# Weight sums of a seven-product matrix multiplication, moved from VectorE to accumulating DMAs

## The chip, the cores and the metric

The kernel runs on one core of one Trainium2 chip. The metric is the time of one execution on the device, in microseconds (us). The engines are TensorE (PE, with its weight loads shown apart as PEld), VectorE (DVE), ScalarE (ACT), GpSimd (POOL) and SyncE (SP), which issues the DMAs of the kernel before. The trace has one profiled execution; its rows are in us or ns.

## What is computed

The reference is block attention over 16 heads' worth of (2, 8, 768, 64) queries, keys and values, and then two feed-forward layers on the 1536 resulting rows of 512:

```python
attn = softmax([local window of 16 | block maxima of k + log 32]) @ [v | block means of v]
x = attn.transpose(0, 2, 1, 3).reshape(1536, 512)
g, val = x @ w_gate, x @ w_val                 # 512 -> 1536
y = (g * sigmoid(g) * val) @ w_out             # 1536 -> 512
h = y @ w_in                                   # 512 -> 2048
out = piecewise(h) @ w_out2                    # h, 0 or (h + 1)^2 / 4;  2048 -> 512
```

The weights come as 64-bit floats and are decoded on the chip to float32. Each float32 product is made of three matmuls: an operand is split into a rounded high part and a low part (value minus high part), and high x high, high x low and low x high are added.

## The kernel before

The 1536 rows are worked on in three chunks of 512. A planner (`Plan.emit`, lines 127 on) takes jobs with needs, buffer rings, engine costs and a rank, and emits them one after the other: always the ready job with the least start time plus 0.00016 x rank. So the constants in `T` set the order on every engine, and each engine then runs its own queue in that order. Where the planner expects PE to idle, `bank` puts padding transposes of `ident` ahead of a job (line 296).

Attention runs first (0 to some 175 us), mixed with the layers of chunk 0, which use the ordinary form (to 265 us). Decoded weights are written to DRAM (`kept_g`, `kept_i` and others). The first products of either layer for chunks 1 and 2 (`JOINT`) are then made together by a seven-product form: the two chunks and two halves of the inner dimension give 2x2 blocks, and seven block products with sums of blocks take the place of eight. Stage 1 has six groups of weights (gate and value columns), stage 2 has four; a group has two quads (e = 0, 1) of seven forms of six matmuls each.

For one group, `read_group` (line 1193) loads a buffer `wj` of 128 x 2 x 4 x 256 values in two DMAs, and `add_group` (line 1208) makes a buffer `sj` of the same size, four sums of 128x512 on DVE, by the table `SUMS` in line 1206: first 0 and 2 from the loaded blocks, then 1 from sum 0, then 3 from sum 1. `wj` and `sj` share a ring of three buffers (`raw`). `group_hi` and `group_lo` (lines 1220, 1226) split both into high and low parts (`wjo` from the plain blocks, `wjs` from the sums; a ring of four, `wA`). PE's job `form` (line 1306) multiplies them with the blocks of x and their differences (`TERMS`, line 1265, split by `term_hi` and `term_lo`) and `fork` and `join` (lines 1318, 1322) build the outputs from the seven products. The second products of each layer (`row_jobs`, tile `acc_y`) use row weights that are read back from DRAM (`wf`, line 1411) and split; they can run at any time after their hidden values are there, so the planner fills PE with them.

Of the kernel before, what the change touches and what calls it, by code (L numbers as in the profile page):

```python
# [23 lines left out]
T = {'rings': {'sm': 4, 'raw': 3, 'dd': 2, 'wf': 3, 'wA': 4, 'h': 3},  # L24
 'handoff': 0.3,
 'urge': 0.00016,
 'weight': (0.925, 772.894, 0.282, 0.289),
 'order': ((0, 1), (0, 2)),
 'pack': 2,
 'ahead': '',  # L30
 'd': (-5637.212, 41085.045),
 'load': (3008.479, 4747.053),
 'high': (-2836.042, 3239.532),
 'bits': (-935.349, 1886.602),
 'keep': (-57947.518, -5594.531),
 'read': -11449.662,
 'hi': (-27701.488, 1102.421),
 'lo': (-11590.763, -2406.109),
 'head_rank': (5076.154, -7290.563, -60395.485, -15458.656),
 'half_rank': -29616.131,  # L40
 'start': 464.292,
 'unit': 1.932,
 'e0': 462.563,
 'a1': (62.363, 14.301),
 'a2': (116.213, 16.636),
 'x': (617.322, 3982.825),
 'j': (2797.217, 10463.422),
 'g': (1.248, 6.748),
 'q': (0.007, 0.113),
 'jr': (1234.441, 846.231),  # L50
 'jw': (1404.409, 766.537),
 'rw': 858.964,
 'js': (-6034.078, 1900.145),
 'gh': (746.555, 1544.378),
 'gl': -1712.874,
 't': 484.136,
 'th': 822.2,
 'tl': -35.6,
 'qp': (-30.096, -19.417, -3.899, 35.81, 32.684, -24.767, -40.513),
 'qf': -562.767,  # L60
 'qj': -1653.995,
 'qa': 2416.954,
 'rs': 3036.454,
 'rh': 887.986,
 'x2': 255.064,
 'r2': (400.241, 30033.282),
 'first': (-5645.576, -144.845),
 'st_q': (-2034.21, 345.71),
 'st_qt': (-732.561, -1914.119),
 'st_sc': (-685.966, -444.589),  # L70
 'st_mx': (-35663.85, -1356.97),
 'st_ex': (-3778.03, 3307.182),
 'st_iv': (-5276.379, 81.698),
 'st_no': (742.266, -11947.766),
 'st_wt': (-4363.695, 165.258),
 'st_pt': (-52297.254, -1058.814),
 'st_av': (-394.819, -213.378),
 'st_xh': (133.16, 1680.548),
 'st_xl': (-10069.461, -3131.586),
 'kl': (-42181.744, 4874.082),  # L80
 'kp': (3666.397, -5596.737),
 'kt': (-3814.781, -1844.408),
 'km': (-77721.471, 514.179),
 'kc': (2433.202, -51674.2),
 'vl': (-198.108, 134.248),
 'vm': (2794.065, -1853.404),
 'vs': 26403.355,
 'vo': (-29543.71, -26442.98),
 've': (-15678.039, 5229.978),
 'ql': (-31980.946, -7672.979),  # L90
 'wl': (-16312.191, -27195.823),
 'wide': 4,
 'st_su': (-4928.084, -22611.06),
 'seg': (-751.648, 28.239),
 'ko': (-4507.859, 33394.294)}


class Plan:
# [28 lines left out]
    def emit(self):  # L127
# [22 lines left out]
        while ready:  # L150
            best = None
            for name in ready:
                engines, rank, fn, needs, takes, gives, after, _ = jobs[name]
                chosen, start0 = [], after
                for group in takes:
                    times = [(t, i) for i, r in enumerate(group)
                             if (t := free_at(r, chosen.count(r))) is not None]
                    if not times:
                        break
                    now = max(start0, max((end[x] for x in needs), default=0.0))  # L160
                    early = [i for t, i in times if t <= now]
                    t, i = (0.0, early[0]) if early else min(times)
                    start0 = max(start0, t)
                    chosen.append(group[i])
                if len(chosen) < len(takes):
                    continue
                way = None
                for kind, us in engines.items():
                    engine, port = kind.strip("+"), kind == "POOL" or kind[-1] == "+"
                    start = max(start0, free.get(engine, 0.0))  # L170
                    if engine == "DMA":
                        us = us[0]
                    elif engine == "PE":
                        now = name[0] in self.TILED
                        start += self.SWITCH * (small and not now) + self.LEAD * (now and not small)
                    if port:
                        start = max(start, free.get("port", 0.0))
                    if engine == "DMA" and len(landed) >= self.LANES:
                        start = max(start, landed[-self.LANES])
                    for x in needs:  # L180
                        start = max(
                            start, end[x] + (self.HANDOFF if done_on[x] != engine else 0.0)
                        )
                    cost = start + self.WEIGHT.get(kind, 0.0) * us
                    if way is None or cost < way[0]:
                        way = cost, start, engine, us, port
                _, start, engine, us, port = way
                late = start + self.URGE * rank
                if best is None or late < best[0]:
                    best = late, start, name, engine, us, port, chosen  # L190
# [9 lines left out]
            if engine == "DMA":  # L200
                us, size, parts = jobs[name][0]["DMA"]
                at = start
                for _ in range(parts):
                    if len(landed) >= self.LANES:
                        at = max(at, landed[-self.LANES])
                    at += us / parts
                    free["moved"] = max(at + self.DMA_START, free.get("moved", 0.0)) + size / parts
                    landed.append(free["moved"] + self.DMA_END)
                free["DMA"], end[name] = at, landed[-1]
            elif engine == "PE":  # L210
                small = name[0] in self.TILED
            done_on[name] = engine
# [19 lines left out]
def tile_block_attention_ffn(  # L232
# [24 lines left out]
    P = 128  # L257
# [945 lines left out]
                    out=t[:, j].rearrange("p (u b) x -> p u (b x)", u=2),  # L1203
                    in_=kept["i", 4 * i + 2 * j])

    SUMS = {0: (0, 1, ALU.add), 2: (2, 0, ALU.subtract), 1: (4, 2, ALU.subtract), 3: (3, 5, ALU.subtract)}

    def add_group(st, i, s, engine):
        w = plain[st, i]
        if s == 0:  # L1210
            sums[st, i] = wp.tile(
                [P, 2, 4, 256], F32, tag="raw", name="sj", bufs=plan.rings["raw"])
        both = [w[:, :, x] if x < 4 else sums[st, i][:, :, x - 4] for x in SUMS[s][:2]]
        nc.vector.tensor_tensor(
            sums[st, i][:, :, s], *both, op=SUMS[s][2])

    def group_source(what, st, i, e):
        return plain[st, i][:, e, 1:4] if what == "o" else sums[st, i][:, e]
# [11 lines left out]
    def group_jobs(st, i, t):  # L1230
        names = [("keep", *group_units(st, i, 0)), ("keep", *group_units(st, i, 1))]
        if st == 1:
            names = [("keep", "g", 2 * i), ("keep", "g", 2 * i + 1)]
        n = (st, i)
        behind = [("load", len(packs) - 1) if n == (1, 0) else ("js", *prior_group, 0)]
        prior_group[:] = n
        job(("ja", *n), {"DMA": (0.8, 2.8, 2)}, t, lambda *_: read_group(st, i), names, (("raw",),),
            follows=behind)
        for s, (x, y, _) in SUMS.items():
            needs = [("ja", *n)] + [("js", *n, z - 4) for z in (x, y) if z >= 4]  # L1240
            job(("js", *n, s), {"DVE+": 0.7}, t + T["js"][st - 1],
                lambda e, *_, s=s: add_group(st, i, s, e), needs, (("raw",),) if s == 0 else (),
                follows=[("js", *n, 0)] if s == 2 else [])
        for e in range(2):
            for what, us in (("o", (0.86, 0.57, 0.97)), ("s", (1.07, 0.7, 1.23))):
                needs = [("ja", *n)] if what == "o" else [("js", *n, s) for s in SUMS]
                gives = ([(("ja", *n), 0)] if what == "o" else [(("js", *n, 0), 0)])
                m = (what, *n, e)
                rank = t + T["q"][st - 1] * e + T["gh"][what == "s"]
                job(("gh", *m), {"ACT": us[0], "DVE+": us[1]}, rank,  # L1250
                    lambda eng, *_, a=m: group_hi(*a, eng), needs, (("wA",),),
                    follows=prior("gh", ("gh", *m)) or [("hi", len(packs) - 1)])
                job(("gl", *m), {"DVE+": us[2]}, rank + T["gl"],
                    lambda eng, a=m: group_lo(*a, eng), [("gh", *m)], (), gives)

        for s in (1, 3):
            jobs = plan.jobs["js", *n, s]
            plan.jobs["js", *n, s] = (*jobs[:5], jobs[5] + ((("ja", *n), 0),), *jobs[6:])

    def operand(st, k, b):  # L1260
# [2 lines left out]
        return parts_of[st, k, b]  # L1263

    TERMS = {
        3: ((C2, 0), (C1, 0)), 5: ((C2, 1), (C2, 0)), 4: ((C2, 1), 3), 6: ((C1, 1), 4),
    }

    def add_term(st, k, b, engine, ring):
# [6 lines left out]
    def term_hi(st, k, b, engine):  # L1276
        if (st, k) not in xts:
            xts[st, k] = big.tile([P, 7, 2, CH], F32R, tag=f"big{k}", name=f"xj{k}")
        copy(engine, xts[st, k][:, b, 0], operand(st, k, b))

    def term_lo(st, k, b, engine):
        t = xts[st, k]
        subtract(engine, t[:, b, 1], operand(st, k, b), t[:, b, 0].bitcast(F32))

    def term_jobs(st, k, t, before, slots):
# [34 lines left out]
        copy(engine, t, quads[q, "a"])  # L1320

    def join(q, what, src):
        nc.vector.tensor_tensor(quads[q, what], quads[q, what], quads[q, src], op=ALU.add)

    def quad_jobs(q, t, slots):
        st, i, e = q
# [163 lines left out]
```

## Time and profile before

| | us |
|---|---|
| median of three runs (614.2 to 615.57) | 614.93 |
| span of the profiled execution | 612.5 |
| PE busy in it | 600.7 |
| DVE busy | 502.4 |
| ACT busy | 347.4 |
| POOL busy | 26.8 |

Busy time of PE counts matmuls back to back; matmuls overlap, so the mean length of one (some 389 ns) is longer than its share of busy time. The granted clock is given as a part of full speed: 1.00 is 2.4 GHz, 0.50 is 1.2 GHz. The DMA share is the mean busy share of the 16 DMA engines; it can pass 1 by rounding of the packets' times.

### The profile page before, as it was taken

What the parts mean: (1) busy time and instruction counts of PE and PEld (TensorE: products, weight loads), DVE (VectorE), ACT (ScalarE), POOL (GpSimd) and SP (SyncE); (2) the same over time, 40 slices, a digit from 0 to 9 for tenths busy, and PEclk for the clock granted to TensorE, in tenths of its full rate; (3) what the DMA queues carried; (4) which work ended last, traced back from release to release, by engine and by line L of the source; (5) the groups of instructions that cost most, each with busy time, mean ns of one, the idle gap of its engine ahead of it and who ended that gap; (6) DMA issues with size and microseconds to landing.
All of it is one profiled execution on the core that took longest, in us unless ns stands there. A gap on an engine that the chain in (4) does not pass through costs nothing.

```text
span 612.5 us, 9841 instructions
## 1 busy us (share of the span) xinstructions
PE 600.7 (98%) x3737; PEld 498.4 (81%) x3737; DVE 502.4 (82%) x910; ACT 347.4 (57%) x634; POOL 26.8 (4%) x54
## 2 busy tenths in 40 slices
PE   8699999999999999999999999999999999999997
PEld 7589888778888888888888888888888888888886
DVE  4788999989899898887788877788888897886662
ACT  5787687877979576454443433322268554742112
POOL 3320201000000000000000000000000000000000
PEclk9979999999999999999999999999999999999999
DMA  8999996999896398132110211123300131103411
GB/s 228 291 303 279 328 303 251 327 266 317 315 339 206 138 307 309 71 139 68 70 68 1 103 70 68 35 104 102 138 20 16 34 138 35 36 0 116 160 35 69
DMA packets 79199, 95.01 MB, mean 155 GB/s; under 512 B 36272, under 2 KB 62128, under 8 KB 79152
## 3 DMA queue, kind: packets, MB, share of 16 engines
q1 hardware_dynamic: 79152, 94.39, 47.9%
q8 instruction: 29, 0.48, 0.3%
q14 instruction: 18, 0.15, 0.1%
HBM read 73.40 MB, written 20.97 MB: 154 GB/s over the span
## 4 chain that ended last, share of the span: by engine, by line
PE 96%; DMA 1%; SPq 1%; ACT 1%; POOL 0%; issue 0%; ACTq 0%; POOLq 0%
PE acc_y L987 38%; PE qi L987 12%; PE qv L987 9%; PE qg L987 9%; PE pi L987 7%; PE pv L987 6%; PE pg L987 6%; PE px L588 2%; PE sc L637 2%; PE pt L683 1%; DMA raw<-in_moe_w_val_dram 1%; PE pk L518 1%; SPq L442 1%; PE pq L569 1%; PE pk L296 1%; SPq L884 1%
## 5 line engine op out<-in xcount | busy, mean ns | idle before, releaser
L987 PE MATMUL acc_y<-dd,h 128*128 128x512 f32 (+1 forms) x387 | 88.4, 387 | 0.0
L987 PEld LDWEIGHTS acc_y<-dd,h 128*128 128x128 f32 x387 | 72.4, 188 | 14.9
L987 PE MATMUL acc_y<-h,dd 128*128 128x512 f32 x288 | 66.1, 389 | 0.0
L987 PEld LDWEIGHTS acc_y<-h,dd 128*128 128x128 f32 x288 | 54.1, 188 | 11.2
L385 ACT ACTIVATE dd<-wf 128x1024 fp32r<-128x1024 f32 x25 | 26.4, 1057 | 61.3 <-PE acc_y L987 61.3
L987 PE MATMUL qi<-xj,wjs 128*128 128x512 f32 x192 | 46.4, 389 | 0.0
L987 PE MATMUL acc_y<-wA,h 128*128 128x512 f32 x192 | 45.8, 389 | 0.0
L903 DVE SCALAR_TENSOR_TENSOR wb<-dd 128x1024 int32<-128x1024 int32 x34 | 41.6, 1227 | 2.3 <-ACT dd L385 1.4
L926 DVE TENSOR_TENSOR wA<-wb,wA 128x1024 fp32r<-128x1024 f32 x34 | 41.6, 1231 | 1.8 <-ACT wA L385 1.1
L987 PE MATMUL pi<-y,wA 128*128 128x512 f32 x128 | 42.4, 392 | 0.0
L987 PEld LDWEIGHTS qi<-xj,wjs 128*128 128x128 f32 x192 | 36.0, 188 | 7.5
L987 PEld LDWEIGHTS acc_y<-wA,h 128*128 128x128 f32 x192 | 36.0, 188 | 7.5
L894 ACT ACTIVATE dd<-raw 128x1024 f32<-128x1024 f32 x34 | 38.8, 1144 | 1.4 <-DMA raw<-in_moe_w_val_dram 1.3
L987 PE MATMUL acc_y<-h,wA 128*128 128x512 f32 x144 | 36.5, 399 | 0.0
L987 PE MATMUL qg<-xj,wjs 128*128 128x512 f32 x144 | 36.4, 389 | 0.0
L987 PE MATMUL qv<-xj,wjs 128*128 128x512 f32 x144 | 36.2, 389 | 0.0
L987 PE MATMUL pg<-x,wA 128*128 128x512 f32 (+1 forms) x112 | 35.2, 371 | 0.0
L987 PE MATMUL qi<-xj,wjo 128*128 128x512 f32 x144 | 34.9, 389 | 0.0
L926 DVE TENSOR_TENSOR dd<-wf,dd 128x1024 fp32r<-128x1024 f32 x28 | 34.2, 1224 | 0.3 <-ACT dd L385 0.2
L987 PE MATMUL pv<-x,wA 128*128 128x512 f32 (+1 forms) x112 | 34.3, 369 | 0.0
L926 DVE TENSOR_TENSOR h<-r,h 128x512 fp32r<-128x512 f32 x47 | 32.4, 692 | 2.1 <-ACT h L385 0.7
L385 ACT ACTIVATE dd<-raw 128x1024 int32<-128x1024 uint32 x28 | 31.9, 1140 | 0.0
(163 smaller groups left out, 1198.8 us busy)
## 6 DMA issues: line engine op xcount, KB each, us to landing
raw<-in_moe_w_out_dram SPq DMA_DIRECT2D x14, 1024.0 KB, 6.3
raw<-in_moe_w_in_dram SPq DMA_DIRECT2D x16, 512.0 KB, 7.3
wf<-kept_z SPq DMA_DIRECT2D x16, 512.0 KB, 3.2
raw<-in_moe_w_gate_dram SPq DMA_DIRECT2D x12, 512.0 KB, 7.1
raw<-in_moe_w_val_dram SPq DMA_DIRECT2D x12, 512.0 KB, 7.6
kept_g<-wb SPq DMA_DIRECT2D x12, 512.0 KB, 5.6
wj<-kept_g SPq DMA_DIRECT2D x12, 512.0 KB, 4.3
wf<-kept_o SPq DMA_DIRECT2D x12, 512.0 KB, 3.2
```

The costliest lines, as they stand in the source:

```text
L296: nc.tensor.transpose(t[:, 0:P], ident, ident)
L385: nc.scalar.activation(out, in_, AF.Copy, scale=scale)
L442: nc.sync.dma_start(out=vwin[0:KW, w], in_=bass.AP(src.tensor, src.offset, [[D, KW], [S * D, H], [1, D]]),)
L518: nc.tensor.matmul(cols[h * D:(h + 1) * D, r], kraw[b, p][one, h, r], ident[one, one], start=True, stop=True, skip_group_check=True)
L569: nc.tensor.transpose(pq[:, r * P:(r + 1) * P], raw[:, r].rearrange("p h d -> p (h d)"), ident)
L588: nc.tensor.matmul(px[h * D:(h + 1) * D, col:col + QT], vwin[0:KN, w, 2 * p + h], pT[0:KN, 2 * h + w // 2, w % 2 * QT:(w % 2 + 1) * QT], s ...
L637: nc.tensor.matmul(scs[h][j * QT:(j + 1) * QT, w // 2], qT[head, (w + j) * QT:(w + j + 1) * QT], kwin[p][head, s * WPS + w + j], start=Tru ...
L683: nc.tensor.transpose(pt[0:KN, w * P:(w + 1) * P], v_["sm"][:, w], ident)
L894: nc.scalar.activation(x[:, 0], raws[k][:, :, :, 1].bitcast(F32), AF.Prelu, scale=2.0 ** -112, alpha=2.0 ** 32)
L903: nc.vector.scalar_tensor_tensor(b, x[:, 0], 3, x[:, 1], op0=ALU.logical_shift_left, op1=ALU.bitwise_or)
L926: e.tensor_tensor(out, a, b, op=ALU.subtract)
L987: nc.tensor.matmul(dst, lhs(a), rhs(b), start=first and i == 0, stop=last and i == 2, **more)
```

## The change

The sums of a group are no longer made on DVE. `read_sums` loads the starting values of `sj` from DRAM with SP's queue (4 DMAs in stage 1, 8 in stage 2), and `add_group` issues from POOL's queue one accumulating DMA per sum that adds a block of `wj` or an earlier sum in place. Since such a DMA only adds, differences are turned into sums: the signs go to the x blocks (terms 0 and 2 are negated, term 5 is turned around) and to the joins. The job `js` becomes an entry of its own in the planner (`SWD`), and nearly all constants of `T` are others.

```diff
+            elif engine == "SWD":
+                at = start + us + self.DMA_START
+                free["moved"] = max(at, free.get("moved", 0.0)) + jobs[name][0]["SWD"][1]
+                end[name] = free["moved"] + self.DMA_END
...
-    SUMS = {0: (0, 1, ALU.add), 2: (2, 0, ALU.subtract), 1: (4, 2, ALU.subtract), 3: (3, 5, ALU.subtract)}
+    SUMS = {0: 1, 2: 0, 1: 4, 3: 5}
+
+    def read_sums(st, i):
+        t = sums[st, i] = wp.tile(
+            [P, 2, 4, 256], F32, tag="raw", name="sj", bufs=plan.rings["raw"])
+        for s, (j, z) in enumerate(((0, 0), (1, 0), (1, 0), (1, 1))):
+            part = slice(256 * z, 256 * z + 256)
+            if st == 1:
+                nc.sync.dma_start(out=t[:, :, s], in_=kept["g", 2 * i + j][:, :, part])
+                continue
+            for e in range(2):
+                nc.sync.dma_start(out=t[:, e, s], in_=kept["i", 4 * i + 2 * e][:, j, part])
+
+    def add_group(st, i, s):
+        x = SUMS[s]
+        nc.gpsimd.dma_start(
+            out=sums[st, i][:, :, s],
+            in_=plain[st, i][:, :, x] if x < 4 else sums[st, i][:, :, x - 4], accum_op=ALU.add)
...
-        for s, (x, y, _) in SUMS.items():
-            needs = [("ja", *n)] + [("js", *n, z - 4) for z in (x, y) if z >= 4]
-            job(("js", *n, s), {"DVE+": 0.7}, t + T["js"][st - 1],
-                lambda e, *_, s=s: add_group(st, i, s, e), needs, (("raw",),) if s == 0 else (),
-                follows=[("js", *n, 0)] if s == 2 else [])
+        job(("jb", *n), {"DMA": (1.6 * st, 1.6 * st, 4 * st)}, t + T["js"][st - 1],
+            lambda *_: read_sums(st, i), names, (("raw",),), follows=[("ja", *n)])
+        for s, x in SUMS.items():
+            needs = [("ja", *n), ("jb", *n)] + ([("js", *n, x - 4)] if x >= 4 else [])
+            job(("js", *n, s), {"SWD": (1.2, 1.2)}, t + T["js"][st - 1],
+                lambda e, s=s: add_group(st, i, s), needs)
...
-        3: ((C2, 0), (C1, 0)), 5: ((C2, 1), (C2, 0)), 4: ((C2, 1), 3), 6: ((C1, 1), 4),
+        3: ((C2, 0), (C1, 0)), 5: ((C2, 0), (C2, 1)), 4: ((C2, 1), 3), 6: ((C1, 1), 4),
...
-        copy(engine, xts[st, k][:, b, 0], operand(st, k, b))
+        copy(engine, xts[st, k][:, b, 0], operand(st, k, b), -1.0 if b in (0, 2) else 1.0)
 
     def term_lo(st, k, b, engine):
         t = xts[st, k]
+        if b in (0, 2):
+            nc.vector.scalar_tensor_tensor(
+                t[:, b, 1], operand(st, k, b), -1.0, t[:, b, 0].bitcast(F32),
+                op0=ALU.mult, op1=ALU.subtract)
+            return
...
-        nc.vector.tensor_tensor(quads[q, what], quads[q, what], quads[q, src], op=ALU.add)
+        t = quads[q, what]
+        if what == "u2":
+            nc.vector.scalar_tensor_tensor(t, t, -1.0, quads[q, src], op0=ALU.mult, op1=ALU.subtract)
+        elif what == "s1":
+            nc.vector.tensor_tensor(t, quads[q, src], t, op=ALU.subtract)
+        else:
+            nc.vector.tensor_tensor(t, t, quads[q, src], op=ALU.add)
```

Of the constants, those that weigh the engines and some of the ranks that the prediction speaks of:

```diff
- 'weight': (0.925, 772.894, 0.282, 0.289),
+ 'weight': (0.935, 3248.959, 0.334, 0.207),
- 'load': (3008.479, 4747.053),
+ 'load': (3040.175, 4777.003),
- 'jr': (1234.441, 846.231),
+ 'jr': (364.158, 292.817),
- 'first': (-5645.576, -144.845),
+ 'first': (-5979.904, 282.679),
- 'vl': (-198.108, 134.248),
+ 'vl': (-1507.519, -2239.376),
- 'wl': (-16312.191, -27195.823),
+ 'wl': (-12671.815, 7162.137),
```

## Rows read from the trace of the kernel before

**Rows 1.** The page: busy us, share, instructions of each engine; the chain that ended last.

```profile
PE 600.7 (98%) x3737; PEld 498.4 (81%) x3737; DVE 502.4 (82%) x910; ACT 347.4 (57%) x634; POOL 26.8 (4%) x54
...
PE 96%; DMA 1%; SPq 1%; ACT 1%; POOL 0%; issue 0%; ACTq 0%; POOLq 0%
```

**Rows 2.** Windows: from:to, length, busy us (instructions) by engine, PE clock, DMA, GB/s.

```profile
24.00:32.00 8.00, 2.22 (x37) 1.19 (x35) 6.19 (x14) 7.48 (x22) 0.00 (x0) 0.88 1.09 352
32.00:36.00 4.00, 3.98 (x32) 3.65 (x33) 3.46 (x8) 2.74 (x4) 0.45 (x1) 0.50 1.11 342
36.00:608.70 572.70, 572.65 (x3246) 474.41 (x3244) 480.35 (x824) 322.77 (x569) 16.44 (x15) 1.00 0.45 148
265.80:386.90 121.10, 121.10 (x536) 100.32 (x535) 98.89 (x141) 52.92 (x82) 2.59 (x2) 1.00 0.21 73
445.40:544.70 99.30, 99.30 (x440) 82.25 (x439) 85.28 (x125) 63.14 (x97) 1.29 (x1) 1.00 0.13 43
```

**Rows 3.** Timeline of PE, 24 to 36 us: start, length, instructions [idle before].

```profile
28.86 0.41 PE L486 MATMUL pv<-vrest,big 128*32 128x128 f32 x4 [3.78 <-DMA vrest<-in_v_dram]
...
32.02 3.03 PE L296 MATMUL px<-ident 128*128 128x128 f32 x13 [1.59 <-ACT big L385]
```

**Rows 4.** Groups by line: DVE's sums (ns min/median/max), a fused form, a scaled copy.

```profile
L1214 DVE TENSOR_TENSOR sj<-wj x20: 684/685/692, 234.9 to 508.8; 128x512 f32<-128x512 f32 x20
L1214 DVE TENSOR_TENSOR sj<-sj,wj x10: 683/684/689, 237.5 to 511.4; 128x512 f32<-128x512 f32 x10
L1214 DVE TENSOR_TENSOR sj<-wj,sj x10: 691/692/694, 238.2 to 512.1; 128x512 f32<-128x512 f32 x10
...
L1053 DVE SCALAR_TENSOR_TENSOR r<-qu,r 128x512 f32<-128x512 f32 x16 | 10.6, 685 | 0.0
...
L391 DVE TENSOR_SCALAR dd<-raw 128x1024 int32<-128x1024 uint32 x6 | 5.2, 862 | 0.4 <-DMA raw<-in_moe_w_val_dram 0.4
```

**Rows 5.** DMAs: KB each, us to landing; wj's issue (ns); SP's longest wait.

```profile
wj<-kept_g SPq DMA_DIRECT2D x12, 512.0 KB, 4.3
...
out_dram<-o SPq DMA_DIRECT2D x11, 256.0 KB, 2.5
...
vrest<-in_v_dram SPq DMA_DIRECT2D x6, 256.0 KB, 7.1
...
L1198 SPq DMA_DIRECT2D wj<-kept_g x12: 518/600/719, 230.5 to 339.1; - x12
...
SPq L1411 <- DVE dd L926: 194.0, 22, 24.3
```

**Rows 6.** POOL's subtractions, and a DVE cast beside one of them (timelines and groups).

```profile
L926 POOL TENSOR_TENSOR h<-u,h 128x512 fp32r<-128x512 f32 x4 | 5.2, 1305 | 194.3 <-DVE h L926 123.1 <-ACT h L385 50.3 <-DVE h L389 20.9
...
473.91 1.29 POOL L926 TENSOR_TENSOR h<-r,h 128x512 fp32r<-128x512 f32 x1 [167.36 <-DVE r L1053]
...
474.02 1.59 DVE L389 CAST wjo<-wj 128x768 fp32r<-128x768 f32 x1
...
L389 DVE CAST wjo<-wj x4: 552/560/1592, 460.4 to 516.2; 128x768 fp32r<-128x768 f32 x4
```

**Rows 7.** Timelines of DVE, ACT and PE for group 2 of stage 1.

```profile
287.36 0.95 DVE L926 TENSOR_TENSOR wjo<-wj,wjo 128x768 fp32r<-128x768 f32 x1
288.35 1.29 DVE L1214 TENSOR_TENSOR sj<-wj 128x512 f32<-128x512 f32 x2
...
301.33 1.06 ACT L385 ACTIVATE wjs<-sj 128x1024 fp32r<-128x1024 f32 x1
...
303.83 1.22 DVE L926 TENSOR_TENSOR wjs<-sj,wjs 128x1024 fp32r<-128x1024 f32 x1
...
306.51 1.52 PE L987 MATMUL qg<-xj,wjs 128*128 128x512 f32 x6
```

**Rows 8.** The chain that ended last: start, length, what; row products of stage 1.

```profile
286.27 1.36 PE acc_y L987 x6
...
386.91 58.51 PE acc_y L987 x258
```

More of the change, by code (lines that the diff above doesn't have):

```diff
@@ L30 @@
  'ahead': '',
- 'd': (-5637.212, 41085.045),
- 'load': (3008.479, 4747.053),
[L33 to L40, printed above, removed]
+ 'd': (6801.398, 16968.89),
+ 'load': (3040.175, 4777.003),
+ 'high': (-3102.001, 3209.872),
+ 'bits': (-2831.968, 2581.436),
+ 'keep': (3914.333, -10248.903),
@@ L41 @@
+ 'read': 3002.138,
+ 'hi': (-3245.898, 502.691),
+ 'lo': (-11177.038, -3252.72),
+ 'head_rank': (3895.343, -3545.831, -11233.838, -31558.917),
+ 'half_rank': -5286.523,
  'start': 464.292,
- 'unit': 1.932,
- 'e0': 462.563,
+ 'unit': 1.539,
+ 'e0': 666.108,
  'a1': (62.363, 14.301),
[L45 to L49, printed above, removed]
- 'jr': (1234.441, 846.231),
- 'jw': (1404.409, 766.537),
- 'rw': 858.964,
- 'js': (-6034.078, 1900.145),
@@ L54 @@
[L54 to L66, printed above, removed]
- 'first': (-5645.576, -144.845),
[L68 to L84, printed above, removed]
- 'vl': (-198.108, 134.248),
[L86 to L89, printed above, removed]
@@ L90 @@
- 'ql': (-31980.946, -7672.979),
- 'wl': (-16312.191, -27195.823),
+ 'a2': (105.973, 18.854),
+ 'x': (968.882, 3077.895),
+ 'j': (3988.874, 11598.947),
+ 'g': (0.899, 12.223),
+ 'q': (0.005439804929925151, 0.09),
+ 'jr': (364.158, 292.817),
+ 'jw': (-3092.825, -507.755),
+ 'rw': 1612.761,
+ 'js': (7989.815, -16462.847),
+ 'gh': (498.458, 1894.373),
+ 'gl': -357.683,
+ 't': 321.576,
+ 'th': 1758.451,
+ 'tl': 175.229,
+ 'qp': (-465.909, -61.92, -780.781, 110.866, -1852.229, -87.975, -450.037),
+ 'qf': -1933.292,
@@ new lines @@
+ 'qj': -804.772,
+ 'qa': 1963.161,
+ 'rs': 1700.064,
+ 'rh': -2270.44,
+ 'x2': -25.702,
+ 'r2': (1279.435, -2777.257),
+ 'first': (-5979.904, 282.679),
+ 'st_q': (-1915.179, 278.921),
+ 'st_qt': (-1912.577, 553.234),
+ 'st_sc': (-130.623, -454.262),
+ 'st_mx': (-82905.053, -5.942),
+ 'st_ex': (-4857.19, 2320.894),
+ 'st_iv': (-5833.239, 56.963),
+ 'st_no': (208.12, -1353.251),
+ 'st_wt': (-6243.042, 90.684),
+ 'st_pt': (-18791.042, -4160.008),
+ 'st_av': (-805.236, -213.378),
+ 'st_xh': (655.97, 3325.77),
@@ L92 @@
+ 'st_xl': (-8516.227, -8571.473),
+ 'kl': (-50473.671, 2823.776),
+ 'kp': (3366.483, -3988.77),
+ 'kt': (-3786.138, 6015.668),
+ 'km': (-22737.891, 232.245),
+ 'kc': (2386.267, -41781.721),
+ 'vl': (-1507.519, -2239.376),
+ 'vm': (3517.73, -6485.962),
+ 'vs': 4619.77,
+ 'vo': (-3388.01, -6653.259),
+ 've': (-32667.048, -861.226),
+ 'ql': (-42675.056, -6717.957),
+ 'wl': (-12671.815, 7162.137),
  'wide': 4,
- 'st_su': (-4928.084, -22611.06),
- 'seg': (-751.648, 28.239),
- 'ko': (-4507.859, 33394.294)}
+ 'st_su': (-4068.273, 1738.361),
@@ L98 @@
+ 'seg': (-1081.344, 21.529),
+ 'ko': (1929.648, -23823.099)}
 class Plan:
@@ L170, in emit @@
                     start = max(start0, free.get(engine, 0.0))
-                    if engine == "DMA":
+                    if engine in ("DMA", "SWD"):
                         us = us[0]
@@ L1204, in read_group @@
                     in_=kept["i", 4 * i + 2 * j])
-    SUMS = {0: (0, 1, ALU.add), 2: (2, 0, ALU.subtract), 1: (4, 2, ALU.subtract), 3: (3, 5, ALU.subtract)}
[L1208 to L1215, printed above, removed]
+    SUMS = {0: 1, 2: 0, 1: 4, 3: 5}
[14 more added lines that the diff above has]
+            in_=plain[st, i][:, :, x] if x < 4 else sums[st, i][:, :, x - 4], accum_op=ALU.add)
     def group_source(what, st, i, e):
@@ L1234, in group_jobs @@
         n = (st, i)
-        behind = [("load", len(packs) - 1) if n == (1, 0) else ("js", *prior_group, 0)]
+        behind = [("load", len(packs) - 1) if n == (1, 0) else ("jb", *prior_group)]
         prior_group[:] = n
@@ L1246, in group_jobs @@
                 needs = [("ja", *n)] if what == "o" else [("js", *n, s) for s in SUMS]
-                gives = ([(("ja", *n), 0)] if what == "o" else [(("js", *n, 0), 0)])
+                gives = ([(("ja", *n), 0)] if what == "o" else [(("jb", *n), 0)])
                 m = (what, *n, e)
@@ L1254, in group_jobs @@
                     lambda eng, a=m: group_lo(*a, eng), [("gh", *m)], (), gives)
-        for s in (1, 3):
+        for s in (0, 2):
             jobs = plan.jobs["js", *n, s]
```

## The prediction

> **What bounds the kernel now.** I read the busy time of each engine first. TensorE (PE) is busy 600.7 of 612.5 us, VectorE (DVE) 82%, ScalarE (ACT) 57%, GpSimd (POOL) 4% [rows 1]. Then the chain that ended last: 96% of it is PE [rows 1]. Then the same busy times by stage [rows 2], to see where PE is not full. From 36 us to the last matmul at 608.7 it is busy 572.65 of 572.70 us. The two stages that use the seven-product form are 265.8 to 386.9 and 445.4 to 544.7: PE is busy 121.10 of 121.10 us and 99.30 of 99.30, at a granted clock of 1.00 (2.4 GHz). DVE is at 98.89 and 85.28 there, so it has room of 22 and 14 us, and no PE wait is put down to it. What is not matmul lies at the ends. Between 24 and 32 us PE is busy 2.22 of 8 us, and from 32 to 36 us it runs at a granted clock of 0.50 (1.2 GHz) after that idle stretch. The tail after that is 612.5 - 608.7 = 3.8 us [rows 2]. The early gap is a wait for data: PE waits 3.78 us for the v rows, then 1.59 us for an ACT copy, and then 13 padding transposes of 3.03 us run before the first px matmul [rows 3]. The DMA engines are at 1.09 and 1.11 of their time meanwhile [rows 2], so these waits are for bytes.
>
> The profiled execution spans 612.5 us and the median of the runs shown is 614.93, so 2.4 us lie around the span; I add them to every span.
>
> **What is removed.** Forty DVE sums, 20 at 685 ns and two kinds of 10 at 684 and 692 [rows 4]: 13.7 + 6.8 + 6.9 = 27.4 us of DVE time. They start between 234.9 and 512.1, where PE does not stop. Worth on the path: 0, because PE already runs back to back there. What is late next, once they are gone, is PE itself.
>
> **Signs.** The b = 0 and 2 terms are split with a factor of -1: 8 high parts by a scaled copy, 8 low parts and 20 of the 60 joins by SCALAR_TENSOR_TENSOR in place of TENSOR_TENSOR. The plain form takes 685 ns on 128x512, the fused form 685 on the same shape [rows 4]: 0. A scaled copy on DVE has its nearest row at 862 ns for 128x1024 [rows 4], so 0.43 for 512 columns; even if all 8 were extra work they would be 3.4 us, hidden in the 22 us of DVE room (3.4 if that cover were gone). They replace copies, so I take 0.
>
> **What is added on SP.** Each of ten groups reads its sum buffer's starting values from DRAM: 4 loads in the first stage, 8 in the second, 24 + 32 = 56 more issues and 10 MB. At 600 ns an issue (the wj loads) [rows 5] that is 2.4 us of queue per group in the first stage, up to 4.8 in the second. The DMA engines are at 0.21 and 0.13 there [rows 2]: room. The load waits for the same buffer that the first sum waited for. Behind it on SP stand the next wj load and the row-weight reads (wf); SP itself waits 194.0 us for DVE to free row buffers [rows 5], so this queue has slack, and the row products that need wf can be put off. Cost 0; without slack some 2.4 us once.
>
> **What is added on POOL.** Four accumulating DMAs per group of 256 KB each. Sum 1 waits for sum 0 and sum 3 for sum 1, so three lie in a row, and POOL's queue stands still while it waits. Behind a waiting one stand the few low-part subtractions of h that POOL does (the one at 473.91 among them) [rows 6]; who waits for those is a row product. The planner counts these DMAs as an engine of their own, so it does not see that wait.
>
> No accumulating DMA is in the trace. The bounds of its time from issue to landing are 2.5 us (256 KB store) and 7.1 us (256 KB load while the DMA engines are full) [rows 5]; it can't be below nothing, since bytes must move. I take 4.3, the 512 KB wj load [rows 5], as an accumulation reads two times 256 KB in a stage with the same light traffic.
>
> **How much time the sums have.** Take group 2 of the first stage [rows 7]. Its buffer comes free when the low parts of group 1 end (287.36 + 0.95 = 288.3); four DVE sums follow from 288.35, 2.6 us in all; but the first split of the sums starts at 301.33, its low part at 303.83, and PE first wants them at 306.51. With 1.06 + 1.22 us for the split and 0.5 for hops, the sums may end at 306.51 - 2.8 = 303.7. The window is 15.4 us, of which DVE used 2.6. The new chain: four issues, the last starting after 3 x 0.6 = 1.8 us, landing 4.3 later, 6.1; three accumulations 3 x 4.3 = 12.9; together 19.0, so 3.6 us too long. The planner's own model, in the diff, has 1.2 + 1.6 + 1.2 + 0.1 = 4.1 per accumulation and 1.6 + 1.6 + 1.6 + 0.1 = 4.9 for the loads; with two hand-offs of 0.3 that is 17.8. So it sees 2.4 too long and puts row products, which are needed anyway, before that group: a block of six takes 1.36 us, and a piece of 258 such matmuls stands after the stage [rows 8]. That part costs 0. What it does not see is 19.0 - 17.8 = 1.2 us per late group; for an accumulation of a us, 3a - 11.7. Two cushions stand against it: blocks of 1.36 us round the filling up, 0.7 on average, and the planner allows 0.8 + 1.6 + 2.8 + 0.1 = 5.3 us for the two wj loads that take 0.6 + 4.3 = 4.9 [rows 5], 0.4 on the safe side; 1.1 together, so 0.1 is left, which I call 0. Groups 0 and 1 of either stage are read early, and as buffers turn over every two groups, a delay of PE moves the next trigger with it: of the 4 + 2 other groups half would pay, 3 stalls. Bounds: at 2.5 us the chain is 4.3 + 7.5 = 11.8, inside the window, 0. At 7.1 it is 1.8 + 4 x 7.1 = 30.2, 12.4 more than planned, 3 x 12.4 = 37 us. The row nearest to the new transfer is the 4.3 one, so 0 stands in the forecast.
>
> The Trainium skill (DMA: Bandwidth & Descriptors, Anatomy of one DMA — SWDGE (gpsimd) path) gives 2.0 us + bytes / 436 GB/s for a DMA from GpSimd, an estimate of 2.6 us for this size, which no row here shows for GpSimd. By it three accumulations would take 7.8 us and, with the loads as above, 13.9 in all: never late, the time of the forecast.
>
> **Order.** Nearly every rank constant changes, so the order on all engines does too. Matmuls stay the same in number, so only the gap at 24 to 36 us and the pads can move: 3.78 + 1.59 = 5.4 us of waiting and 3.03 of pads [rows 3]. The loads that set the gap keep their order by their ranks (v windows, weights 0 and 1, v rows), which speaks for about the same start. Sum: 612.5 + 0 + 0 + 2.4 = 614.9.
>
> **Rivals.** *A better start* (0.31): pads fall away, or the v rows come earlier. Without pads, 3.0 us less: 611.9; half of the wait besides: 609. For it: the pads run at half clock ahead of work that could start. Against: the DMA engines are full.
> *Chain late* (0.24): PE waits for the sums in three groups. If the cushions fail at 4.3 us, 3 x 1.2 more: 618.5. If they hold and an accumulation takes 5.0, 3 x (3.3 - 1.1) = 6.6 more: 621.5. It decides from 4.3 us, since 3a - 11.7 passes 1.1 there. For it: two reads and POOL's own work on top of a plain load. Against: the light traffic.
> *POOL held off by DVE* (0.06). At 474.02 a DVE cast took 1.59 us, not the 0.56 of its kind, while POOL ran for 1.29 from 473.91 [rows 6]: one keeps the other out. If each accumulation had to wait for one DVE instruction of 1.22 us [rows 7], the chain would grow by 3.7, and 3 stalls of 3.8 make 11.4: 626.3. The Trainium skill states this (DMA: Bandwidth & Descriptors, SWDGE vs HWDGE vs iDMA): GpSimd writes its descriptors into SBUF, and DVE locks it out while in a two-port mode. The trace agrees only that the two exclude each other; POOL's own four subtractions of this kind took 1305 ns in the mean [rows 6], no longer than the one at 473.91, which gives little weight to it.
> *A worse start or more switches between attention and products* (0.06): 617.
> *Sums don't matter at all and only order acts* would look like the forecast or the first rival; it is told apart by the stage's PE time.
>
> **How the numbers follow.** Forecast 0.33 (613.7 to 616.1), the likeliest; its time is 614.9. This kernel's measurement can tell about 0.2%, 1.2 us. Faster 0.31, same 0.33, slower 0.24 + 0.06 + 0.06 = 0.36. The range takes in all but the lock rival and the far ends: 610.0 to 621.5.
>
> **What would show it.** Right: PE still busy for all of both seven-product stages, no L1214 group on DVE, 40 POOL DMAs landing in about 4.3 us, DVE busy some 27 us less. Chain late: PE waits on DVE or ACT ahead of wjs matmuls, a few us each, in groups 2 and on. Lock: POOL DMA issues far apart while DVE is busy. Start: pads other than 13, idle between 24 and 32 other than 5.8 (8 less 2.22). The forecast is wrong if an accumulation lands later than 5 us, or if the start moves by more than 1.2 us.

## The result and the profile after

The changed kernel takes 618.43 us (median of 11 runs, 615.47 to 625.26); the kernel before takes 614.67 beside it (11 runs, 612.88 to 618.69). The ratio is 1.0058, with a 95% interval of 1.0037 to 1.0079: the change costs some 3.6 us by the ratio (which leaves out the one run of 625.26, over 1.5% above the fastest), where no change had been forecast. The time lies inside the predicted range of 610.0 to 621.5, but above the forecast's own 613.7 to 616.1. The runs of the changed kernel also lie further apart than those of before, and that turns out to be part of the cause.

The profiled execution took 615.81 us, with a span of 614.1, so it is one of the better ones. From its page, the busy time of each engine and the chain that ended last (for before: [rows 1]):

```profile
PE 601.2 (98%) x3740; PEld 498.0 (81%) x3740; DVE 484.2 (79%) x885; ACT 342.7 (56%) x628; POOL 65.1 (11%) x85
...
PE 87%; SPq 3%; DMA 3%; DVE 3%; issue 2%; ACT 1%; POOL 1%; ACTq 0%; DVEq 0%; POOLq 0%
```

PE does the same work. DVE is 18.2 us lighter and not 27, since in the new order it has also taken on more copies (27 casts of `wA` for 22, 15 of `wjo` for 11, and others). POOL is 38.3 us heavier. What was a chain of 96% PE now runs through DMAs, SP's queue and DVE for about a tenth of the span. Windows show where (from:to, length, then busy us of PE, PEld, DVE, ACT and POOL, PE's clock, DMA share, GB/s):

```profile
240.00:260.00 20.00, 20.00 (x90) 16.58 (x89) 18.30 (x25) 8.64 (x11) 3.82 (x3) 1.00 0.97 306
260.00:270.00 10.00, 9.59 (x42) 7.31 (x41) 7.30 (x12) 6.08 (x9) 1.19 (x1) 1.00 0.80 214
270.00:280.00 10.00, 10.00 (x46) 8.29 (x45) 8.66 (x13) 5.19 (x9) 2.42 (x2) 1.00 0.85 251
280.00:400.00 120.00, 120.00 (x531) 99.44 (x530) 89.24 (x128) 45.07 (x67) 26.39 (x22) 1.00 0.66 158
400.00:600.00 200.00, 200.00 (x884) 165.65 (x883) 151.55 (x225) 95.64 (x138) 14.41 (x12) 1.00 0.38 101
```

PE is full in all of them but one: it loses 0.41 us between 260 and 270, where the first seven-product stage begins (PE's first form at 266.27; before at 265.71). In before these 10 us were full too. The DMA share ahead of that place is 0.97; in before the same 20 us had 0.37:

```profile
240.00:260.00 20.00, 20.00 (x90) 16.57 (x89) 17.94 (x28) 8.33 (x13) 0.00 (x0) 1.00 0.37 130
```

Four timelines of that place, one queue or engine each (start, length, engine, line, operation, [idle before, and what ended it]). SP's queue, the loads of `sj` for group 0 and of `wj` for group 1:

```profile
241.84 2.63 SPq L1218 DMA_DIRECT2D sj<-kept_g  x4
245.44 1.17 SPq L1202 DMA_DIRECT2D wj<-kept_g  x2
```

POOL, the four sums of group 0:

```profile
246.73 2.62 POOL L1225 DMA_DIRECT2D sj<-wj  x2 [84.87 <-DMA sj<-kept_g]
257.71 1.19 POOL L1225 DMA_DIRECT2D sj<-sj  x1 [8.36 <-DMA sj<-wj]
262.80 1.19 POOL L1225 DMA_DIRECT2D sj<-sj  x1 [3.89 <-DMA sj<-sj]
```

DVE:

```profile
266.74 0.69 DVE L393 CAST wjs<-sj 128x1024 fp32r<-128x1024 f32 x1 [2.42 <-DMA sj<-sj]
267.35 0.55 DVE L393 CAST wjo<-wj 128x768 fp32r<-128x768 f32 x1
267.93 0.96 DVE L930 TENSOR_TENSOR wjo<-wj,wjo 128x768 fp32r<-128x768 f32 x1
```

PE:

```profile
266.27 1.52 PE L991 MATMUL qg<-xj,wjo 128*128 128x512 f32 x6
267.95 0.73 PE L991 MATMUL qv<-xj,wjo 128*128 128x512 f32 x2 [0.15 <-DVE wjo L393]
268.94 1.20 PE L991 MATMUL qv<-xj,wjo 128*128 128x512 f32 x4 [0.26 <-DVE wjo L930]
```

Read from the bottom up: PE waits for a split of plain blocks (`wjo`), which needs no sum at all. That split stands on DVE behind the split of the sums (`wjs`), which stands still for 2.42 us until the last accumulating DMA has landed. And that DMA is the end of a chain that began with the loads of `sj` at 241.84 on SP's queue and lasted 24.9 us.

DMAs by kind (KB each, median us from issue to landing; for before: [rows 5]):

```profile
wj<-kept_g SPq DMA_DIRECT2D x12, 512.0 KB, 6.6
sj<-kept_g SPq DMA_DIRECT2D x24, 256.0 KB, 4.2
wf<-kept_o SPq DMA_DIRECT2D x12, 512.0 KB, 6.9
sj<-wj POOLq DMA_DIRECT2D x20, 256.0 KB, 8.5
sj<-sj POOLq DMA_DIRECT2D x20, 256.0 KB, 3.8
```

The same kind of transfer has two prices. A sum that waits for another sum (`sj<-sj`) runs with less beside it and lands in 3.8 us. The first two sums of a group (`sj<-wj`) go out together, beside the next group's loads, and land in 8.5. The loads of `wj` take 6.6 us where they took 4.3; the experiments show whether that comes from the new sums.

The theory to be tested: the whole loss is the chain of group 0 in stage 1, which ends too late and holds up PE through DVE's queue. Its rivals: the new order of the jobs costs the time; the 56 extra loads or the lighter DVE do; the other groups' sums are late too; POOL's DMAs are held off by DVE.

### The profile page after: what moved, and what is told of

Same layout as the page of the kernel before. It is cut to its first block, busy times and chain, and to the rows that moved or that the text cites. A ratio compares the mean times of both kernels' runs of the same rounds, so it can differ in the third digit from the quotient of the medians.

```text
span 614.1 us, 10017 instructions
## 1 busy us (share of the span) xinstructions
PE 601.2 (98%) x3740; PEld 498.0 (81%) x3740; DVE 484.2 (79%) x885; ACT 342.7 (56%) x628; POOL 65.1 (11%) x85
## 3 DMA queue, kind: packets, MB, share of 16 engines
q0 software_dynamic: 10880, 10.49, 11.2%
## 4 chain that ended last, share of the span: by engine, by line
PE 87%; SPq 3%; DMA 3%; DVE 3%; issue 2%; ACT 1%; POOL 1%; ACTq 0%; DVEq 0%; POOLq 0%
PE acc_y L991 34%; PE qi L991 12%; PE qv L991 9%; PE qg L991 9%; PE pg L991 6%; PE pv L991 6%; PE pi L991 5%; PE px L592 2%; SPq L446 2%; PE sc L641 1%; PE pt L687 1%; DMA raw<-in_moe_w_val_dram 1%; DMA sj<-kept_g 1%; DMA sj<-sj 1%; POOL sj L1225 1%
## 5 line engine op out<-in xcount | busy, mean ns | idle before, releaser
L1225 POOL DMA_DIRECT2D sj<-wj x20 | 24.2, 1224 | 214.7 <-DMA sj<-kept_g 106.3
L907 DVE SCALAR_TENSOR_TENSOR wb<-dd 128x1024 int32<-128x1024 int32 x34 | 43.1, 1271 | 1.5 <-ACT dd L389 0.6
L393 DVE CAST h<-r 128x512 fp32r<-128x512 f32 x46 | 19.6, 427 | 24.7 <-PE acc_y L991 23.6
```

What stands on the lines that cost most here:

```text
L393: nc.vector.tensor_copy(out, in_)
L907: nc.vector.scalar_tensor_tensor(b, x[:, 0], 3, x[:, 1], op0=ALU.logical_shift_left, op1=ALU.bitwise_or)
L1225: nc.gpsimd.dma_start(out=sums[st, i][:, :, s], in_=plain[st, i][:, :, x] if x < 4 else sums[st, i][:, :, x - 4], accum_op=ALU.add)
```

## The experiments

Ratios are to runs of the kernel before on the same chip. "In the changed kernel" means that nothing else was edited.

**The changed kernel again.** No edit.

> The changed kernel as it is, for a second look at its scatter (615.5 to 622 us between its runs, where before has 612.9 to 615.6). Theory late sums: a run above 617 us shows PE waiting in the seven-product stages, first at the start of stage 1 (some 266 to 270 us), where its queue stood for 0.41 us in the first profile, and the granted clock falls when the wait is long. Theory order: PE is full there in every run, and the scatter lies ahead of 60 us, in the wait for the v rows.

Measured: 618.48 us (9 runs, 615.77 to 621.28), ratio 1.0077 (1.0052 to 1.0101). So the loss repeats. In its profile DVE waits 2.61 us for `sj<-sj`, the split of the sums starts at 268.00, and PE waits 0.61 and 0.26 us for `wjo`, and 0.47 us for an ACT copy at 299.12.

**The old sums with the new constants, and the new sums with the old constants.** In the kernel before, `T` is replaced by the changed kernel's; in the changed kernel, by that of before.

```diff
- 'weight': (0.925, 772.894, 0.282, 0.289),
+ 'weight': (0.935, 3248.959, 0.334, 0.207),
...
```

> The kernel before with only the constants of the changed one: sums on DVE, other ranks. Theory order: the start comes later by 1.1 us as in the changed kernel, 616 to 618 us. Theory late sums: 614.5 to 616 us and a scatter as small as before's.

> The changed kernel with the constants of the one before: accumulating DMAs, old ranks. Theory late sums: slower than before by 2 to 10 us, with PE waits ahead of matmuls with sums. Theory order: the time of before, 614 to 615.5 us.

Measured: 622.49 us, ratio 1.0134 (1.0110 to 1.0157), for old sums with new constants; 624.54 us, ratio 1.0178 (1.0139 to 1.0217), for new sums with old constants. Either crossing is slower than both kernels. The constants are ranks for a certain list of jobs, so with another list the planner makes an order that is neither the one nor the other: these two don't separate order from sums, and the first lies outside what either theory expected. In the first of them DVE makes group 0's sums only from 269.33 on, and PE waits 3.21 us for `wjo`, which stands on DVE behind them: the same stall by another way. The second shows something else. PE's waits from 200 us on (us in all, times, the longest):

```profile
PE qg L991 <- ACT wjs L389: 3.4, 4, 2.1
PE qg L991 <- DVE wjs L930: 2.1, 4, 0.5
```

Here group 0's chain starts earlier (its first sum is issued at 238.95, not 246.73) and PE does not wait for it. Instead it waits for the sums in the later groups, at 287, 334, 359 and 384: this is what the rival "chain late" of the prediction looks like when it is true. The changed kernel's constants cure that, and leave group 0.

**The sums on DVE, in the changed kernel.** The accumulating DMA is replaced by an addition on DVE at the same place in the order, once with the loads of `sj` kept, and once without them (the sum then reads two blocks).

```diff
-        nc.gpsimd.dma_start(
-            out=sums[st, i][:, :, s],
-            in_=plain[st, i][:, :, x] if x < 4 else sums[st, i][:, :, x - 4], accum_op=ALU.add)
+        t = sums[st, i][:, :, s]
+        nc.vector.tensor_tensor(
+            t, t, plain[st, i][:, :, x] if x < 4 else sums[st, i][:, :, x - 4], op=ALU.add)
```

> The changed kernel with its order and its loads of starting values, but each accumulating DMA is one VectorE add in the same place (0.69 us in place of some 4 to 8 us from issue to landing). Theory late sums: the scatter goes, 615 to 616 us. Theory order: 617 to 619 us as the changed kernel. Theory GpSimd lock: as late sums, and DVE's instructions are no longer than with the DMAs only if the two had kept each other waiting.

> As the run with VectorE adds in the accumulations' place, but without the 56 loads of starting values: VectorE adds two blocks of wj. If the loads cost (SP's queue, 10 MB), 613.5 to 614.7 us; if they are hidden as forecast, 615.2 as with them. What is left over the kernel before is then the order alone.

Measured: 615.22 us with the loads, ratio 1.0020 (1.0003 to 1.0036); 615.18 without, ratio 1.0018 (0.9998 to 1.0039). So the accumulating DMAs carry the larger part of the loss: 618.48 less 615.22, some 3.3 us of the 4.9 by which the changed kernel was slower on this chip. With the sums on DVE the 56 loads cost nothing that can be measured (the two ratios differ by 0.0002). What is left is some 1.2 us by these ratios, with intervals that reach down to nothing or nearly so. PE waits nowhere between 40 us and the end in either profile. With the loads, DVE's split of group 0's sums does not wait and starts ahead of PE's first form:

```profile
265.06 0.69 DVE L393 CAST wjs<-sj 128x1024 fp32r<-128x1024 f32 x1
...
265.85 1.52 PE L991 MATMUL qg<-xj,wjo 128*128 128x512 f32 x6
```

The loads of `wj` still take 7.0 us here, and 5.0 without the loads of `sj`. So it is those loads, right ahead of `wj` on SP's queue, that slow `wj`, and not the accumulating DMAs.

**The same DMAs without the addition.** `accum_op` is taken away, so the DMAs copy. The sums are left out of the computation; the chain, its order and the bytes that the queue counts stay.

```diff
-            in_=plain[st, i][:, :, x] if x < 4 else sums[st, i][:, :, x - 4], accum_op=ALU.add)
+            in_=plain[st, i][:, :, x] if x < 4 else sums[st, i][:, :, x - 4])
```

> The changed kernel, but the 40 DMAs from GpSimd copy and don't accumulate (the additions are left out, so sums are not computed). In the changed kernel the first accumulation of a group lands 8.3 us after its issue and the later ones 3.8. If accumulating costs (it reads twice), the copies land in under 3 us and under 5 us and the time falls to 615 to 616 us. If the first one is slow for what moves beside it (the next wj loads, 1 MB, and the second accumulation), copies land as late, within 0.5 us, and the time stays at 618 us.

Measured: 613.90 us, ratio 0.9996 (0.9985 to 1.0008), as fast as before. Two lines of its DMAs by kind, and the line of POOL's DMA queue (packets, MB, share of 16 engines):

```profile
sj<-wj POOLq DMA_DIRECT2D x20, 256.0 KB, 7.1
sj<-sj POOLq DMA_DIRECT2D x20, 256.0 KB, 2.5
...
q0 software_dynamic: 3200, 10.49, 4.6%
```

and the same queue of the changed kernel:

```profile
q0 software_dynamic: 10880, 10.49, 11.2%
```

So the addition costs 1.3 to 1.4 us per DMA, in company (8.5 against 7.1) and out of it (3.8 against 2.5). Neither expectation held whole: the time fell, to below what was expected, but most of the 8.5 us of the first sums stays without the addition. There are three in a row, and POOL's instruction takes 0.72 us in place of 1.20. The chain of group 0 ends early enough: the split of its sums starts at 264.66 with no wait, PE's first form at 266.71. Some 2 us off the chain make the whole difference: what counts is whether it ends ahead of PE's start. The order, the signs, the loads and the lighter DVE are those of the changed kernel, so by themselves none of these four makes the loss.

**The next group's loads behind the sums.** In the changed kernel the loads of `wj` are ordered behind the last sum of the group before; from group 2 of each stage on they go out from POOL's queue.

```diff
-        behind = [("load", len(packs) - 1) if n == (1, 0) else ("jb", *prior_group)]
+        behind = [("load", len(packs) - 1) if n == (1, 0) else ("js", *prior_group, 3)]
```

> The wj loads of groups 2 and on are issued from GpSimd's queue behind the last sum of the group before, so they don't move beside its first accumulations. Theory contention: the first accumulations land in some 4 to 5 us and not 8.3, the chain of a group is 3 to 4 us shorter, 615 to 617 us. If accumulation itself is slow, they stay at 8 and the time is 618 us or more, since wj is loaded later.

Measured: 616.72 us, ratio 1.0037 (1.0020 to 1.0055). SP's queue and POOL's in its profile:

```profile
241.33 2.60 SPq L1219 DMA_DIRECT2D sj<-kept_g  x4
...
256.71 1.38 SPq L1203 DMA_DIRECT2D wj<-kept_g  x2
```

```profile
246.74 2.63 POOL L1226 DMA_DIRECT2D sj<-wj  x2 [85.39 <-DMA sj<-kept_g]
253.89 1.20 POOL L1226 DMA_DIRECT2D sj<-sj  x1 [4.52 <-DMA sj<-wj]
```

With `wj` of group 1 at 256.71 in place of 245.44, the first two sums of group 0 are done 7.15 us after their issue and not 10.98. POOL's wait for them is 4.52, not 8.36. In the other profiles of the changed kernel these two sums took 10.6 to 11.9 us. This shows the company: the loads right behind the sums cost the chain 3.8 us here. The first accumulations landed in 6.2 us by the median, not in the 4 to 5 that were expected. PE no longer waits for `wjo`. The gain is partly spent: a split of x is now late (PE waits 1.3 us for `xj` from DVE), and 0.7 us more in two waits.

**The plain splits first.** The loops over the kinds of split and the quads are swapped in the changed kernel, so that the jobs that need no sum come first in the list.

```diff
-        for e in range(2):
-            for what, us in (("o", (0.86, 0.57, 0.97)), ("s", (1.07, 0.7, 1.23))):
+        for what, us in (("o", (0.86, 0.57, 0.97)), ("s", (1.07, 0.7, 1.23))):
+            for e in range(2):
```

> Both halves' plain blocks are split ahead of the sums (the chain of splits runs o, o, s, s and not o, s, o, s). Theory late sums by way of a queue: at the start of stage 1 DVE waits 2.4 us for the sums with a plain split behind it, and PE for that split; with this order PE doesn't wait there, the wait for sums falls behind the plain forms: 615 to 617 us. If the plan gets worse elsewhere by it, 619 or more, with waits in other groups.

Measured: 623.31 us, ratio 1.0158 (1.0119 to 1.0196); a miss as a cure. PE's waits from 200 us on:

```profile
PE qg L991 <- DVE xj L930: 2.3, 1, 2.3
PE qg L991 <- DVE wjs L393: 0.9, 1, 0.9
...
PE qg L991 <- DVE wjs L930: 0.5, 1, 0.5
```

The wait for `wjo` is gone, as it should be. But the edit moves all groups, and PE then reaches the sums themselves, which are no earlier (the last lands at 269.3), and then an x split. Taking the bystander out of the queue does not help while the sums are late.

**Only group 0 of stage 1 on DVE, and all groups but that one.** In the changed kernel `add_group` adds on DVE for the groups named and keeps the DMA for the rest; the second kernel has `!=` for `==`.

```diff
+        if (st, i) == (1, 0):
+            t = sums[st, i][:, :, s]
+            nc.vector.tensor_tensor(
+                t, t, plain[st, i][:, :, x] if x < 4 else sums[st, i][:, :, x - 4], op=ALU.add)
+            return
```

> The changed kernel, but the four sums of group 0 of stage 1 are VectorE adds in the same place; the other nine groups accumulate. If the loss of late sums sits at the start of stage 1, where the profiles show PE waiting 1.0 to 1.4 us, the time is that of VectorE adds everywhere, 615 to 615.8 us, and the scatter goes. If the other groups are late too, about half of the 3.3 us stays: 616.5 to 618 us.

> The other way round: group 0 of stage 1 accumulates, the nine others are VectorE adds. If the loss sits in group 0: 617.5 to 619 us. If it sits in the others: 615 to 616 us.

Measured: with only group 0's four sums on DVE 615.07 us, ratio 1.0008 (0.9990 to 1.0026), no different from before. With only those four left on DMAs 620.52 us, ratio 1.0105 (1.0075 to 1.0135). So 4 of the 40 accumulating DMAs make the loss, and the other 36 make none that can be told from zero. The second time lies above its expected 617.5 to 619 and above the changed kernel's 618.4 and 618.5. Why is not shown; the first look below, on the same chip, took 620.48. PE at the stage's start in the first of the two:

```profile
267.23 1.52 PE L991 MATMUL qg<-xj,wjo 128*128 128x512 f32 x6
268.59 1.52 PE L991 MATMUL qv<-xj,wjo 128*128 128x512 f32 x6
```

and in the second:

```profile
265.47 1.52 PE L991 MATMUL qg<-xj,wjo 128*128 128x512 f32 x6
269.84 0.73 PE L991 MATMUL qv<-xj,wjo 128*128 128x512 f32 x2 [2.85 <-DVE wjo L393]
```

**Two more looks at the changed kernel.** No edit; one profile each, to see how the stall varies.

> The changed kernel once more, for a profile of another of its executions. Late sums: the more it lies above 615.5 us, the longer PE waits after 266 us, ahead of matmuls whose weights were split behind a wait for sums. Order: the start of stage 1 comes later by as much as the time is longer.

> As the look before: one more execution of the changed kernel, to set the length of the stretch from the first seven-product matmul on against the time.

Measured: 620.48 and 618.57 us. The first caught a long stall: its chain began 0.74 us earlier on POOL (245.99), and each of its links took longer (the last sum is issued at 264.57, not 262.80). DVE, then PE:

```profile
269.56 0.69 DVE L393 CAST wjs<-sj 128x1024 fp32r<-128x1024 f32 x1 [5.98 <-DMA sj<-sj]
```

```profile
265.44 1.52 PE L991 MATMUL qg<-xj,wjo 128*128 128x512 f32 x6
270.77 3.07 PE L991 MATMUL qv<-xj,wjo 128*128 128x512 f32 x6 [3.81 <-DVE wjo L393]
273.64 2.54 PE L991 MATMUL qg<-xj,wjo 128*128 128x512 f32 x6
276.01 1.54 PE L991 MATMUL qg<-xj,wjs 128*128 128x512 f32 x6
```

and a window of the same execution (columns as above):

```profile
270.00:280.00 10.00, 9.22 (x30) 7.14 (x31) 8.87 (x12) 4.55 (x8) 2.38 (x2) 0.71 0.55 165
```

With the wait of 3.81 us comes a granted clock of 0.71 in the 10 us from 270 on; from 270 to 275 it was 0.50, which is 1.2 GHz. The twelve matmuls from 270.77 to 276.01 take 5.24 us; at 1.00, two such sets of six take 2 x 1.36 = 2.72. So the clock costs 2.5 us more. From PE's first form to the end of the span this execution took 618.8 - 265.44 = 353.4 us, before took 612.5 - 265.71 = 346.8; of the 6.6 us between them 3.81 + 2.5 = 6.3 are these two.

The profiles that have group 0 on DMAs, side by side (us):

| profile | loads of `sj` issued | PE's first form | DVE's split of the sums | PE waits for `wjo`, high part | by the rule below | PE's first form to the end |
|---|---|---|---|---|---|---|
| changed kernel | 241.84 | 266.27 | 266.74 | 0.15 | 0.15 | 347.8 |
| the same again | 242.66 | 267.09 | 268.00 | 0.61 | 0.59 | 349.1 |
| look 1 | 241.01 | 265.44 | 269.56 | 3.81 | 3.80 | 353.4 |
| look 2 | 243.89 | 268.31 | 269.34 | 0.72 | 0.71 | 348.6 |
| only group 0 on DMAs | 241.05 | 265.47 | 268.62 | 2.85 | 2.83 | 353.1 |

The rule: PE can use `wjo` 1.2 us after DVE's split of the sums starts (0.61 to the next cast, 0.55 for it, a hop), and needs it 1.52 us after its first form starts. So the wait is the third column less the second, less 0.32. All five agree within 0.02 us.

In all five the loads of `sj` go out 24.4 us ahead of PE's first form: the chain's start and PE's move together, by up to 2.9 us. What sets the stall is how long the chain takes, from the issue of these loads to DVE's split: 24.9 us in the profile of the changed kernel, 28.6 in look 1. Above some 24.7 us PE stalls, and in the two longest chains its clock falls as well. Why the chain takes longer in some executions is not shown.

The last column tells the loss apart from the start. Before it was 346.8 us. With the sums on DVE, with copies, or with only group 0 on DVE it was 346.8 to 347.6, against 347.8 to 353.4 in the table. PE's first form itself comes at 265.4 to 268.3 us in the table and at 264.7 to 267.2 in those others, so this part of the scatter does not come from the sums. Of look 2's time, 2.6 us over before are such a later start. The runs scatter more than before's because the length of the chain comes on top of it.

## Why the prediction was wrong

**What held.** The bound: PE is full from 36 us on in the changed kernel but for the 0.41 us. The sums on DVE are worth nothing on the path that the profiles show: back on DVE, no PE wait comes of them. SP's loads: no difference between with and without, as long as the sums are on DVE. Signs: no stall on an x split in the changed kernel. The start: 24 to 36 us has 13 pads, 1.06 us later than before, and a wait of 3.77 us for the v rows, as in [rows 3]:

```profile
29.49 0.48 PE L490 MATMUL pv<-vrest,big 128*32 128x128 f32 x4 [3.77 <-DMA vrest<-in_v_dram]
...
33.08 3.04 PE L300 MATMUL px<-ident 128*128 128x128 f32 x13 [1.80 <-ACT big L389]
```

The lock: the 40 instructions on POOL take 1191 to 1399 ns beside a DVE that is busy 79% of the time, and no wait of POOL for DVE stands between two sums of a chain. The rule that the prediction drew from the Trainium skill (DMA: Bandwidth & Descriptors, SWDGE vs HWDGE vs iDMA), that DVE can lock GpSimd out while it writes descriptors, has no row here that shows it.

**The later groups.** "So it sees 2.4 too long and puts row products, which are needed anyway, before that group" is what happened in group 2 of stage 1. The sums' issues on POOL, the split on ACT, and PE:

```profile
295.02 1.20 POOL L1225 DMA_DIRECT2D sj<-wj  x1 [7.26 <-DVE qu L1343]
...
307.95 1.20 POOL L1225 DMA_DIRECT2D sj<-sj  x1 [2.86 <-DMA sj<-sj]
```

```profile
311.95 1.05 ACT L389 ACTIVATE wjs<-sj 128x1024 fp32r<-128x1024 f32 x1
```

```profile
313.50 2.88 PE L991 MATMUL acc_y<-h,dd 128*128 128x512 f32 x12
316.22 1.52 PE L991 MATMUL qv<-xj,wjo 128*128 128x512 f32 x6
317.58 1.52 PE L991 MATMUL qg<-xj,wjs 128*128 128x512 f32 x6
```

From the loads' issue at 291.40 to the last landing at some 311.8 the chain took 20.4 us; the forecast worked with 19.0, the planner with 17.8. PE's first use is at 317.58 and not at 306.51 [rows 7], row products fill the place, and PE does not stop. The rival's "three groups" were those that the planner knew about; its filling covered the 20.4 us in this one, where the prediction allowed 17.8 and 1.1 of cushions, and PE waits for sums in none of the later ones.

**The step that failed** is one sentence: "Groups 0 and 1 of either stage are read early". It set the cost of group 0 at nothing. In the kernel before it is so: `wj` goes out from 230.5 on [rows 5], and group 0's four sums start on DVE between 234.9 and 238.2 [rows 4], 27 us and more ahead of PE's first form at 265.71. But how far ahead the new chain would begin was not worked out. In the changed kernel SP's queue reaches the loads of `sj` only at 241.84, 24.4 us ahead of PE's first form. That would do for a chain of 19.0; it does not do for one of 24.9 to 28.6.

**The mis-sized term** is 4.3 us for every accumulation. It measured 8.5, 3.8 and 3.8 by the medians, so two of three terms were near and one was double; the prediction's own sign of being wrong, an accumulation that lands later than 5 us, came true. The row that it was taken from, `wj` in a quiet stage [rows 5], was nearest by bytes but not by company. Group 0's chain runs from 241 to 267, where the decoded weights are still being written and the next group's loads go out: a DMA share of 0.97. Little of that share is the sums' own: with the sums on DVE the same 20 us had 0.87, and 0.66 without the loads of `sj`. The chain's parts were 4.89 us for the loads (the prediction had 6.1), 10.98 for the first two sums, then 5.09 and 3.94 (4.3 each): 24.9 in all. The upper bound in the prediction (7.1 us, a load while the DMA engines are full) was the nearer row for that group. The estimate of 2.6 us that the prediction made by the Trainium skill (DMA: Bandwidth & Descriptors, Anatomy of one DMA — SWDGE (gpsimd) path) agrees with the copies without addition, 2.5 us when little runs beside them, and not with the accumulating form: 3.8 us, and 8.5 in company. Here the measurement decides.

**What was not counted** is DVE's queue. The prediction named who stands behind a waiting instruction on POOL and on SP, but the wait that the change adds ends on the engine that splits the sums. Behind it on DVE stood `wjo`, which PE needed first. So PE stopped at 267.80, 3.5 us before it uses the sums (271.34 in the changed kernel), and that much of the lead was gone.

So the rival "chain late" was right that the sums end too late, and wrong in the place and number: one stall that varies, in group 0, on a split that needs no sum, and not three of a fixed size from group 2 on. What decides is how long group 0's chain takes in the traffic beside its first sums, not whether each accumulation takes more than 4.3 us. That its 618.5 us is nearly the measured time is chance, since it came from three stalls of 1.2 us that did not happen.

**Not tried, and left open.** What keeps the loads of `sj` for group 0 from going out before 241.84: they stand right behind a write of `kept_i` at 241.41 on SP's queue, and with the old constants they went 9.6 us earlier, but then the later groups stall. A kernel with group 0's sums on DVE reaches the time of before, and none of the versions run here beats it: with PE full there is nothing for the freed DVE time to buy. The versions with all sums on DVE may have some 1 us over before, which these runs hardly tell from zero. The copies, with the same order, signs and loads, have none (0.9996), so it would not be order and signs alone; its cause stays open.

## What to carry to other kernels

Moving work from an engine with room to a chain of DMAs gained nothing here, where another engine is the bound, and turned 2.6 us of latency into 20 to 29; so check the start of each stage by itself, where nothing has been worked ahead and the traffic is at its highest. Price a DMA by a row with the same company, not only the same bytes, and count what stands behind the waiting consumer on its in-order queue, even if it needs nothing of the transfer. When runs of a kernel scatter more than before, look for two chains that end close together.

## What the runs showed of the hardware

An accumulating DMA of 256 KB was cut into 10880 / 40 = 272 packets, the same transfer as a copy into 3200 / 40 = 80. It cost POOL 1.20 us to issue, not 0.72, and landed in 3.8 us, not 2.5. The DMA engines' share of POOL's queue rose from 4.6% to 11.2% for the same 10.49 MB counted. Of the loads beside them, `wf<-kept_o` took 3.4 us with the sums on DVE and no loads of `sj`, 4.7 with those loads, 6.9 with the accumulating DMAs besides and 6.8 with copies in their place. `wj<-kept_g` took 5.0, 7.0, 6.6 and 7.2 us in the same four kernels, so the accumulating DMAs added nothing to it.

In look 1, with a PE wait of 3.81 us, the 10 us from 270 on had a mean granted clock of 0.71; in the kernel with only group 0 on DMAs, with a wait of 2.85 us, it was 0.83. In the three other profiles of the changed kernel, with waits there of 0.98 us or less in all, it stayed at 1.00.
